# Gated mix of a long convolution and dilated local attention: x's first piece, the value weights and v loaded in other pieces, with a new written-out order

## The chip, the cores and the metric

The kernel runs on one core of a Trainium2 chip. A core has a matrix engine (TensorE, PE in the views; its weight loads are PEld), three engines for elementwise work (VectorE or DVE, ScalarE or ACT, GpSimd or POOL), a queue engine (SyncE or SP), and 16 DMA engines that move data between the chip's memory and the core's 128-partition buffer. Every engine works through its own instructions strictly in program order and waits on semaphores; a DMA is issued by SP, ACT or POOL and raises a semaphore when it has landed. The metric is device microseconds of one execution, as the median of several runs.

## What is computed

```python
x = A_q                                           # (1, 2048, 640), bf16
g = sigmoid((x * gate_w).sum(-1, keepdims=True))
# a: k is convolved with 4 taps, multiplied by v, and convolved over all 2048 positions
kv = sum_t(k shifted by t * shift_k[:, t]) * v
y  = irfft(rfft(kv, 4096) * rfft(ssm_k, 4096))[:2048] + kv * ssm_D
a  = A_q * y
# b: 32 heads of 20, each position sees itself and 7 earlier ones, every second position
q, k_, v_ = split(x @ wqkv)
b  = softmax(q . k_[pos - 2 * (0..7)] / sqrt(20)) . v_ @ wo
out = g * a + (1 - g) * b
```

## The kernel before, in words

**Attention.** x is loaded transposed (`load_x`, line 291) into `xT`, positions split by parity `par` into two halves of 1024, since the window has a dilation of 2. Each `load_x` is one transposing DMA of 512 rows, so x comes in four pieces x00, x01, x10, x11. `vproj` (line 437) multiplies pieces of 121 positions by the value weights `Wv`, once for the first 16 heads (columns 0 to 319 of `Wv`, hf 0) and once for the other 16 (hf 1). `qkproj` makes queries and keys, evicts them to `stg`, and `fragger` issues small DMAs from POOL (line 537, `qb<-stg`, `kb<-stg`, here called fragments) that put the heads where `score_gen` needs them. `score_gen` (scores, exp on ACT) and `pv_gen` (weighted values, normalised on DVE, lines 597 and 600) go through eight groups of four heads.

**Long convolution.** The channels lie on partitions in four quarters `q` of 32 partitions; partition 32q+p holds positions 64p to 64p+63 of the channels that start at CH[q] (CH = 0, 320, 160, 480). A quarter's 160 channels are two halves `c` of 80. k is loaded by eight DMAs into `kin`, v by eight DMAs into `vin[32q:32q+32, c]` (one for each q and c), the long filter by sixteen into `h_lin`. `conv` (line 410, its products on line 401 and its sums on line 408) is the 4-tap convolution on DVE, in place in `kin`. `conv_v` (line 426) then multiplies it by v in four DVE instructions, two for c = 0 and two for c = 1, on all 128 partitions: those of one c wait for all loads of that c. After that come two matmul stages for h and for kv (`transform`: `s1_unit`, line 621, and `s2_unit`, line 637), the product in the frequency domain (`products`), two inverse stages and the gating.

**Order.** All instructions are written out in an order made beforehand: `ORDER` is a string in which each letter lets one generator (a = `loads`, b = `fragger`, g = `conv_v`, v and w = `vproj` for the two halves of heads, and so on) emit its next request; `ENGINES` says which engine takes an eviction that ACT or DVE could take. The numbers in the requests (durations, landings, `plan.at`) are what the search for the order used; at run time they do nothing. An engine's queue follows the order even when a later instruction could already run.

**Pacing.** The loads of v and of the long filter are `paced` (line 286): POOL writes one element per partition of the destination first (line 288), and the DMA waits for that. So the place of that memset among POOL's fragments sets when SP may issue the load, and everything behind it on SP waits too. SP's order in `loads` (line 298) is x00, x01, W0 (query weights), x10, W1 (key weights), x11, eight k, eight v, sixteen h. The DMA of v on line 283 has this source, four times for each c:

```python
raw(v2, CH[q] + 80 * c, [[64 * D, 32], [D, 64], [1, 80]])      # [step, count], outermost first
```

The same helper builds the source of `g_nat` (line 466), the four small loads that spread the gate's row over partitions: `[[32 * pt, 2], [32, 16], [1, 32]]` for 32 destination partitions.

`heads` (line 357) emits what comes before the ordered part: two DMAs on ACT's queue for `Wv` (128-row blocks 0 to 2, then 3 and 4), `mm` (the mask rows), `ident` (for the transposes on line 755), the copies of the mask rows into key set 0 and query set 0 (`masks`, lines 354 and 355) on ACT, memsets on DVE, twelve warm-up matmuls, and small loads on POOL, `F` last among them.

Of the kernel before, what the change touches and what calls it, by code (L numbers as in the profile page):

```python
# [17 lines left out]
S = 2048  # L18
D = 640
# [7 lines left out]
BQ = 114  # L27
# [3 lines left out]
PRE = 7  # L31
X0 = 16
HS = 1024
HP = HS + 16
# [11 lines left out]
QC = 160  # L46
CR = 11
WARM = 12
CH = [0, 320, 160, 480]
# [61 lines left out]

STREAMS = "abcdefghijklmnopqrstuvwxyzABCDEFGHIJKLMNOPQRSTUVWXYZ"
ORDER = """
aaaaaaaaaaavwwwvvwvvvwwwvfaiviwvwviiiaweaiwvwvveeiibeiibwbwevveeivieeewwvvewbbbbbbbbbabwaeiiicecbibieecieccceacibcbcacbiebiacceccibbaidbcicc
bccbbbcabeediaieeiicbccbcbcciceicbbdccaabebcidccbbcaccdbeicccicdeieeabccccidbiacdcbceibcccecacieiciccbbbbbdbabbbacacaeccaaaadaicibabccbcacec
cddicicccecceeiiebieicbeacacecdcaceccibbdbddibiabeccciacjbjbccaggcbciabbcigacciccbcjccdicgcajjjaclcidbcihdccacbdccickialczzzccczacczckzzzccd
cczdzbbbbbbzbbbbbccbjazzczcccazbcacdbdcczzccczczkczzdccccczcjdczccczczkccaaazcazdaaacckcdkczcclzzczklzzzmzkzccdcAzccdzczAAAAAAAdAdnAAAzAzzAz
AAAAAABAppCpBBBABBABBBBBAABBCCBBBBkkkkkkkBkBBoABACAACCCCCAAAAAAAAAAACACACAoCCoCoCoooBoCopBooCoooCpCpCBpBBpCxBBpCCCxBxppCqCxBBxBBBqoBBqoCBBCo
xCBBBxxxxoCxxqqqqqxqkBCBCxxCxCqqCokxxxooooooooxxxoCCDykCCCCCqqqqqqqrqyqqrrrrDDrDDDDDDDyDDDDDyyDyDDyyyyyyyyyyyyyryyysDDEErEEEErrDEEEEEssErrEE
rrrrEsEEEEEskEsqqrrrtrttttttttttttttttttttttttttttttqqtstqttqqqqttqtstttttqqttuuuuuuuuuuuuuuuuuuuuuuuuuuuu  # L120
"""
ENGINES = """
DADADAADADDDADDAAAAADAAADAAAAAAADDAADADAAAADDDDDDDADADDDDADDDDDAADADADAADAADDAADADAADADADADADAADADADADADADADADADADAADAAADAADADADAAAAADAAADAA
AAAAAAAAAAAAAAADAAADAAADDDADDADADDAADAADASSSSSSSSSSSSSSSSSSSSSASSASAS
"""


# [50 lines left out]
def kernel(  # L178
# [14 lines left out]
    nc = tc.nc  # L193
# [6 lines left out]
    def raw(ap, off, dims):  # L200
        return bass.AP(tensor=ap.tensor, offset=ap.offset + off, ap=dims)
# [9 lines left out]
    plan = Plan(4)  # L211
# [48 lines left out]
    def ev(name):  # L260
        if name not in E:
            E[name] = Ev()
        return E[name]

    def mark(name, g):
        x = ev(name)
        x.t, x.eng = g.done.t, g.done.eng

    def at(name, t):
        ev(name).t = t  # L270
# [10 lines left out]
    def load(name, dst, src, us, deps=()):  # L281
        g = yield Req("S", 520.0, deps, move=us)
        nc.sync.dma_start(dst, src)
        mark(name, g)

    def paced(name, dst, src, us, deep=False):
        g = yield Req("G", 200.0)
        nc.gpsimd.memset(dst[:, 0, 0, 0:1] if deep else dst[:, 0, 0:1], 0.0)
        yield from load(name, dst, src, us, [g.done])

    def load_x(par, h, us):
        g = yield Req("S", 2700.0, move=us)
        nc.sync.dma_start_transpose(xT[:, :, X0 + HP * par + 512 * h:X0 + HP * par + 512 * h + 512],
                                    raw(x2, (1024 * h + par) * D, [[2 * D, 512], [1, D]]))
        mark(f"x{par}{h}", g)

    def loads():
        yield from load_x(0, 0, 5200.0)
        yield from load_x(0, 1, 4400.0)
        yield from load("W0", Wqk[:, :, 0, :], W3[:, :, 0, :], 2800.0)  # L300
        yield from load_x(1, 0, 2600.0)
        yield from load("W1", Wqk[:, :, 1, :], W3[:, :, 1, :], 3900.0)
        yield from load_x(1, 1, 3700.0)
        for c in (1, 0):
            for q in range(4):
                yield from load(f"k{q}{c}", kin[32 * q:32 * q + 32, 3 + 32 * c:35 + 32 * c, :],
                                raw(k2, 32 * c * D + CH[q], [[64 * D, 32], [D, 32], [1, QC]]), 2000.0)
        for c in range(2):
            for q in range(4):
                yield from paced(f"v{q}{c}", vin[32 * q:32 * q + 32, c], raw(v2, CH[q] + 80 * c, [[64 * D, 32], [D, 64], [1, 80]]), 2450.0)  # L310
        h_lin = p0.tile([128, 80, 2, 64], BF, name="h_lin", tag="HL")
        st["h_lin"] = h_lin
        for P in range(2):
            for q in range(4):
                for c in range(2):
                    yield from paced(f"h{P}{q}{c}", h_lin[32 * q:32 * q + 32, PL * P:PL * P + PL, c, :],
                                     raw(A_ssm_k, (CH[q] + 80 * c + PL * P) * S, [[64, 32], [S, PL], [1, 64]]), 1200.0)
# [37 lines left out]
        copier(qsets[e][:].rearrange("p (b k) -> p b k", k=BQ), mm[:, BK:BK + BQ].unsqueeze(1).to_broadcast([128, NB, BQ]))  # L355

    def heads():
        nc.scalar.dma_start(Wv[:, 0:3], W3[:, 0:3, 2, :])
        nc.scalar.dma_start(Wv[:, 3:5], W3[:, 3:5, 2, :])
        nc.scalar.dma_start(mm[:], ca["mm"].ap())  # L360
        nc.scalar.dma_start(ident[:], ca["ident"].ap())
        masks(nc.scalar.copy, 0)
        z = pab[:, 0].rearrange("p n c -> p (n c)")
        nc.vector.memset(z, 0.0)
        nc.vector.memset(ETall[:, :, :, 3 * BQ:], 1.0)
        nc.vector.memset(VW[:, :, :, DH], 1.0)
        for j in (0, NBP):
            nc.vector.memset(VW[0:PRE, j, :, DH], 0.0)
        wu = psp.tile([128, 2, 512], F32, name="wu", tag="ps0")
        for n in range(WARM):  # L370
            nc.tensor.matmul(wu[:, n % 2, :], lhsT=z[:, 0:128], rhs=z[:, 0:512], start=True, stop=True, skip_group_check=True)
        nc.gpsimd.memset(wgz[:], 0.0)
        nc.gpsimd.memset(xT[:, :, 0:X0], 0.0)
        for c in range(2):
            nc.gpsimd.memset(xT[:, :, X0 + HP * c + HS:X0 + HP * (c + 1)], 0.0)
        nc.gpsimd.dma_start(wgz[:, :, 0], gate_w.rearrange("(t p) -> p t", p=128))
        nc.gpsimd.memset(Dz[:], 0.0)
        for q in range(4):
            nc.gpsimd.dma_start(Dz[32 * q:32 * q + 1, :], raw(A_ssm_D, CH[q], [[0, 1], [1, 160]]))
        for q in range(4):  # L380
            nc.gpsimd.memset(kin[32 * q:32 * q + 1, 0:3, :], 0.0)
            nc.gpsimd.dma_start(wraw[32 * q:32 * q + 32].rearrange("p c j -> p (c j)"), raw(A_shift_k, 4 * CH[q], [[0, 32], [1, 4 * QC]]))
        masks(nc.gpsimd.tensor_copy, 1)
        for q in range(4):
            for a, b in ((1, 17), (17, 32)):
                nc.gpsimd.dma_start(kin[32 * q + a:32 * q + b, 0:3, :], raw(k2, (64 * a - 3) * D + CH[q], [[64 * D, b - a], [D, 3], [1, QC]]))
        nc.gpsimd.dma_start(F[:], cf["F"].ap())
        plan.at["A"] = 13500.0
        plan.at["G"] = 18500.0
        plan.at["P"] = 5500.0  # L390
        at("Wv0", 6500.0)

    def xdeps(par, i0, i1):
        return [ev(f"x{par}{h}") for h in range(2) if i0 < 512 * h + 512 and i1 > 512 * h]

    X4 = [f"x{par}{h}" for par in range(2) for h in range(2)]

    def taps(eng, n, m, ta, tb, dst):
        def tap(d, j):
# [24 lines left out]
    def conv_v():  # L424
        for c in range(2):
            for n in (0, 32):
                g = yield Req("D", 150.0 + 0.525 * 32 * 80, [ev("convD")] + [ev(f"v{q}{c}") for q in range(4)])
                nc.vector.tensor_tensor(vin[:, c, n:n + 32, :], kin[:, n + 3:n + 35, 80 * c:80 * c + 80], vin[:, c, n:n + 32, :], ALU.mult)
        mark("convV", g)

# [4 lines left out]
    def vproj(hf):  # L435
        for u in range(NBP):
            pieces = [divmod(2 * u + i, NBP) for i in range(2)]
            g = yield Req("P", 5 * 270.0, [d for par, j in pieces for d in xdeps(par, BQ * j - PRE, min(HS, BQ * j + BQ))] + [ev("Wv0")], take=1, mode="f", mm=10)
            ps = psum(g, "psv")
            for i, (par, j) in enumerate(pieces):  # L440
                s0 = X0 + HP * par + BQ * j - PRE
                for dt in range(NDT):
                    nc.tensor.matmul(ps[0:BK, i, 0:320], lhsT=xT[:, dt, s0:s0 + BK], rhs=Wv[:, dt, 320 * hf:320 * hf + 320],  # L443
                                     start=(dt == 0), stop=(dt == NDT - 1))
            r = yield Req("AD", n=640, deps=[g.done], give=g.banks)
            copy(r.eng, VW[0:BK, 2 * u:2 * u + 2, 16 * hf:16 * hf + 16, 0:DH], ps[0:BK, :, 0:320].rearrange("p a (h d) -> p a h d", d=DH))
            for i in range(2):
                mark(f"VW{2 * u + i}h{hf}", r)
        mark(f"vproj{hf}", g)

    def gate():
        g = yield Req("P", 1300.0, [ev(x) for x in X4], take=1, mode="g", mm=20)
        gps = psum(g, "gps", (128, 512))
        for dt in range(NDT):
            for c in range(4):
# [431 lines left out]
```

## Time and profile before

| what | us |
|---|---|
| median of 3 runs (236.31 to 237.9) | 236.75 |
| the profiled execution's own time | 235.22 |
| its span, first to last instruction | 233.1 |
| PE, DVE, ACT, POOL busy | 208.3, 184.5, 168.9, 58.7 |
| first `vproj` matmul | 10.68 |
| v's first and last load issued by SP | 47.2, 78.9 |
| first and last product of `conv_v` on DVE begin | 97.9, 103.7 |

All views are of one profiled execution; times in them count from the span's start. A busy share is over the span or a stretch. "Granted clock" (PEclk) is the share of TensorE's full clock that the chip allowed. In a line of the timeline the first number is the start, the second the time that the entries merged in it reach over.

### The profile page before, as it was taken

How to read it: one execution, taken by the hardware profiler on the slowest of the kernel's cores; microseconds unless marked ns; L12 is line 12 of the kernel's file. 1: busy time of each engine (PE TensorE's matmuls, PEld its weight loads, DVE VectorE, ACT ScalarE, POOL GpSimd, SP SyncE). 2: the span in 40 equal slices, each digit the busy share in tenths (PEclk: the TensorE clock that was granted, in tenths of full speed). 3: DMA queues.
4: the chain of work that ended last, by engine and by line, in shares of the span. 5: the costliest groups of instructions: out<-in, count | busy, mean ns of one | idle time of the engine just before them, and what ended most of it. 6: DMA issues, size and time to landing. Idle time of an engine off the chain costs nothing.

```text
span 233.1 us, 8740 instructions
## 1 busy us (share of the span) xinstructions
PE 208.3 (89%) x3802; PEld 168.2 (72%) x3802; DVE 184.5 (79%) x256; ACT 168.9 (72%) x216; POOL 58.7 (25%) x136
## 2 busy tenths in 40 slices
PE   6299999999899989999899998999999999997930
PEld 2189888866667656666667777888898999996920
DVE  4112269769999999997887779999999999598970
ACT  2432214459798989697999779998997979859950
POOL 8799030445733740742600000000000000000000
PEclk9769999999999999999855589999999999999995
DMA  7999999179699699978699550964767642294754
GB/s 190 221 269 294 167 165 158 36 160 166 115 142 171 128 148 144 145 111 190 119 177 195 172 183 18 211 146 88 172 141 164 158 107 40 56 236 84 184 128 95
DMA packets 74213, 34.91 MB, mean 150 GB/s; under 512 B 59876, under 2 KB 70768, under 8 KB 74176
## 3 DMA queue, kind: packets, MB, share of 16 engines
q1 hardware_dynamic: 69152, 27.50, 62.5%
q0 software_dynamic: 3792, 5.81, 11.9%
q10 hardware_dynamic: 1232, 1.06, 1.9%
q8 instruction: 29, 0.48, 0.9%
q14 instruction: 8, 0.07, 0.1%
HBM read 18.43 MB, written 2.62 MB: 90 GB/s over the span
## 4 chain that ended last, share of the span: by engine, by line
PE 49%; DVE 19%; DMA 10%; issue 9%; ACT 6%; POOL 3%; DVEq 0%; POOLq 0%; ACTq 0%
PE psv L443 10%; PE i L737 8%; PE op L775 7%; PE pj L492 7%; PE s L637 7%; DMA kb<-stg 6%; ACT ETall L567 4%; PE sc L560 4%; DVE Hs L207 4%; DMA wgz<-in_gate_w_dram 3%; DVE UC L207 3%; PE O L588 3%; DVE SX L835 3%; DVE SX L838 3%; PE tr L755 2%
## 5 line engine op out<-in xcount | busy, mean ns | idle before, releaser
L567 ACT ACTIVATE ETall<-sc 121x912 bf16<-121x912 f32 (+1 forms) x80 | 63.9, 863 | 9.2 <-PE sc L560 8.8
L492 PE MATMUL pj<-xT,Wqk 128*128 128x342 bf16 (+1 forms) x300 | 48.3, 310 | 2.6 <-ACT ETall L567 1.2
L492 PEld LDWEIGHTS <-Wqk 128*128 128x128 bf16 x300 | 28.4, 97 | 16.7 <-issue 2.2
L443 PE MATMUL psv<-KX,xT 128*121 128x320 bf16 x180 | 27.9, 318 | 4.2 <-POOL kb L353 4.2
L205 ACT CAST UC<-s 128x960 bf16<-128x960 f32 (+2 forms) x31 | 28.0, 982 | 3.7 <-PE s L637 2.2
L443 PEld LDWEIGHTS <-xT 128*121 128x121 bf16 x180 | 25.8, 144 | 6.0 <-POOL kb L353 4.7
L537 POOL DMA_DIRECT2D qb<-stg x36 | 18.0, 503 | 36.7 <-ACT stg L205 13.0
L401 DVE TENSOR_TENSOR KX<-KX 128x1760 bf16<-128x1760 bf16 (+1 forms) x24 | 24.6, 1044 | 0.5
L205 ACT CAST stg<-pj 128x726 bf16<-128x726 f32 (+1 forms) x17 | 12.8, 758 | 15.7 <-PE pj L492 12.7
L560 PE MATMUL sc<-qb,kb 31*128 31x114 bf16 x576 | 22.7, 229 | 1.6 <-DVE SX L207 0.5
L775 PE MATMUL op<-wo,oT 128*32 128x320 bf16 x640 | 23.9, 302 | 0.1
L637 PEld LDWEIGHTS <-SX 64*128 64x128 bf16 x512 | 20.9, 101 | 3.1 <-issue 2.3
L775 PEld LDWEIGHTS <-oT 128*32 128x32 bf16 x640 | 21.3, 140 | 1.3 <-issue 0.4
L537 POOL DMA_DIRECT2D kb<-stg x36 | 17.9, 502 | 17.0 <-issue 9.7
L560 PEld LDWEIGHTS <-kb 31*128 31x128 bf16 x576 | 13.8, 100 | 11.0 <-issue 9.2
L207 DVE CAST stg<-pj 128x684 bf16<-128x684 f32 (+1 forms) x13 | 11.5, 885 | 11.6 <-PE pj L492 9.2
L408 DVE TENSOR_TENSOR KX<-KX 128x1760 bf16<-128x1760 bf16 (+1 forms) x18 | 18.8, 1043 | 0.3
L207 DVE CAST SX<-s 128x1024 bf16<-128x1024 f32 (+1 forms) x13 | 15.2, 1191 | 3.7 <-PE s L637 2.9
L737 PE MATMUL i<-F,Hw 128*128 128x128 bf16 x160 | 18.0, 219 | 0.0
L737 PEld LDWEIGHTS <-Hw 128*128 128x128 bf16 x160 | 17.9, 113 | 0.0
L588 PEld LDWEIGHTS <-ETall 121*128 121x128 bf16 x576 | 16.2, 97 | 2.3 <-issue 1.0
L588 PE MATMUL O<-VW,ETall 121*128 121x21 bf16 x576 | 17.2, 174 | 0.5 <-DVE stg L207 0.4
(73 smaller groups left out, 339.3 us busy)
## 6 DMA issues: line engine op xcount, KB each, us to landing
KX<-in_A_k_dram SPq DMA_DIRECT2D x8, 320.0 KB
vin<-in_A_v_dram SPq DMA_DIRECT2D x8, 320.0 KB
h_lin<-in_A_ssm_k_dram SPq DMA_DIRECT2D x16, 160.0 KB
Hw<-SX SPq DMA_DIRECT2D x8, 320.0 KB
Hw<-Hs SPq DMA_DIRECT2D x8, 320.0 KB
SX<-in_A_q_dram SPq DMA_DIRECT2D x16, 160.0 KB
kb<-stg POOLq DMA_DIRECT2D x28, 85.1 KB, 3.9
qb<-stg POOLq DMA_DIRECT2D x28, 80.2 KB, 4.7
```

The costliest lines, as they stand in the source:

```text
L205: nc.scalar.copy(dst, src)
L207: nc.vector.tensor_copy(dst, src)
L401: eng.tensor_tensor(d, kin[:, n + 3 - j:n + 3 - j + m, :], w.to_broadcast([128, m, QC]), ALU.mult)
L443: nc.tensor.matmul(ps[0:BK, i, 0:320], lhsT=xT[:, dt, s0:s0 + BK], rhs=Wv[:, dt, 320 * hf:320 * hf + 320], start=(dt == 0), stop=(dt == ND ...
L492: nc.tensor.matmul(ps[:, i, 0:n], lhsT=Wqk[:, dt, w, 128 * ft:128 * ft + 128], rhs=xT[:, dt, s0:s0 + n], start=(dt == 0), stop=(dt == NDT ...
L537: nc.gpsimd.dma_start(dst[r0:r0 + rows, 0:wd], stg[fa - f0:fb - f0, 0:wd])
L560: nc.tensor.matmul(sc[:, hh, BQ * bb:BQ * bb + BQ], lhsT=kb[r:r + DH + NF, BK * b:BK * b + 128], rhs=qb[r:r + DH + NF, BQ * b:BQ * b + BQ] ...
L567: nc.scalar.activation(ETall[0:BK, e, :, 0:BQ * nb], sc[0:BK, :, 0:BQ * nb], ACT.Exp, scale=SCALE)
L588: nc.tensor.matmul(O[:, (b - b0) // 6, c0:c0 + 21], lhsT=ETall[0:BK, e, hh, BQ * bb:BQ * bb + 128], rhs=VW[0:BK, b, 4 * t + h4, :], start= ...
L637: nc.tensor.matmul(ps[:, c, 160 * jj:160 * jj + 160], lhsT=st["G"][rows, j0 + jj, rr, :], rhs=Am[rows, rr].rearrange("p o (q j) l -> p j ( ...
L737: nc.tensor.matmul(d, lhsT=st[(key, P)][:, c, o + il // 4, :, il % 4], rhs=M[:, k, :], start=(k == 0), stop=(k == 1), skip_group_check=True)
L775: nc.tensor.matmul(op[c:c + 32, tt, 0:320], lhsT=oT[:, ft, h, 32 * e:32 * e + 32, a], rhs=wo[:, ft, 320 * w:320 * w + 320], start=(ft == 0 ...
```

## The change

x00 becomes two transposing loads of 256 rows each (x00 and x01; the former x01 is now x02, the former x11 is x12). `Wv` is loaded by halves of heads, columns 0 to 319 first, and `vproj` waits only for its own half. The masks of set 0 are copied on DVE instead of ACT, behind DVE's memsets; `ident` is loaded from POOL's queue, after `F`, instead of ACT's. v comes in four transfers instead of eight, each for two quarters (64 partitions), and the source of each is written with the two quarters outermost. The planned durations, landings and `plan.at` are set anew, and `ORDER` and `ENGINES` come from a new search: 939 letters instead of 946, in `ENGINES` 114 A and 70 D instead of 110 and 74.

```diff
-    def load_x(par, h, us):
-        g = yield Req("S", 2700.0, move=us)
-        nc.sync.dma_start_transpose(xT[:, :, X0 + HP * par + 512 * h:X0 + HP * par + 512 * h + 512],
-                                    raw(x2, (1024 * h + par) * D, [[2 * D, 512], [1, D]]))
-        mark(f"x{par}{h}", g)
+    def load_x(name, par, t0, n, cost, us):
+        g = yield Req("S", cost, move=us)
+        nc.sync.dma_start_transpose(xT[:, :, X0 + HP * par + t0:X0 + HP * par + t0 + n], raw(x2, (2 * t0 + par) * D, [[2 * D, n], [1, D]]))
+        mark(name, g)
...
-        yield from load_x(0, 0, 5200.0)
-        yield from load_x(0, 1, 4400.0)
-        yield from load("W0", Wqk[:, :, 0, :], W3[:, :, 0, :], 2800.0)
...
+        yield from load_x("x00", 0, 0, 256, 2000.0, 2800.0)
+        yield from load_x("x01", 0, 256, 256, 2400.0, 3000.0)
+        yield from load_x("x02", 0, 512, 512, 4800.0, 4000.0)
+        yield from load("W0", Wqk[:, :, 0, :], W3[:, :, 0, :], 2400.0)
...
         for c in range(2):
-            for q in range(4):
-                yield from paced(f"v{q}{c}", vin[32 * q:32 * q + 32, c], raw(v2, CH[q] + 80 * c, [[64 * D, 32], [D, 64], [1, 80]]), 2450.0)
+            for q in (0, 2):
+                yield from paced(f"v{q}{c}", vin[32 * q:32 * q + 64, c], raw(v2, CH[q] + 80 * c, [[320, 2], [D, 2048], [1, 80]]), 3500.0)
...
     def heads():
-        nc.scalar.dma_start(Wv[:, 0:3], W3[:, 0:3, 2, :])
-        nc.scalar.dma_start(Wv[:, 3:5], W3[:, 3:5, 2, :])
+        for hf in range(2):
+            nc.scalar.dma_start(Wv[:, :, 320 * hf:320 * hf + 320], W3[:, :, 2, 320 * hf:320 * hf + 320])
         nc.scalar.dma_start(mm[:], ca["mm"].ap())
-        nc.scalar.dma_start(ident[:], ca["ident"].ap())
-        masks(nc.scalar.copy, 0)
...
+        masks(nc.vector.tensor_copy, 0)
...
         nc.gpsimd.dma_start(F[:], cf["F"].ap())
+        nc.gpsimd.dma_start(ident[:], ca["ident"].ap())
...
-                g = yield Req("D", 150.0 + 0.525 * 32 * 80, [ev("convD")] + [ev(f"v{q}{c}") for q in range(4)])
+                g = yield Req("D", 150.0 + 0.525 * 32 * 80, [ev("convD")] + [ev(f"v{q}{c}") for q in (0, 2)])
```

In the new order the four v loads are issued behind 13, 16, 32 and 37 requests of `fragger`; the eight of before behind 13, 17, 21, 27, 32, 37, 41 and 50. The four products of `conv_v` stand behind 80, 85, 87 and 93 requests of `score_gen`; before, behind 86, 86, 89 and 97.

More of the change, by code (lines that the diff above doesn't have):

```diff
@@ L113 @@
 ORDER = """
[L114 to L120, printed above, removed]
+aaaaavaaaaavvvawaawawvwvawvvwwviivvwiiwiiiiwiwwbeibeeeewwevewbvwibiwvvbbbebvbvvebeibwbabaiiiieicbbcaceecciecccbiifaiecbccbcbebiicccdccbcbbcb
+bibbecbbedbiibeideccciadeciccceicbeicacccicicccedccecebcdbbiibacbccabbadeccbbcccicdiccacbicbicccdccbbcicbceeeeedeicbabacdiecdcbbiccciaeeiaea
+becccaaabbeicaacbabaiccdccbaccajaicabebeeebjiibdgdciclabccadbbbiicbgccabaagbiccjjcjccliicgcaccjdhbickcccicdizaczcazbccdaccdczacaccbabzzbbbcb
+bcbbbbbzbczzzaacdcclzccccdzczcdcczckcdclckzzczczczzzccdccdczczzczkkczzkccczczcczzmzzzkczdccccdczzcAccAAAckdkcAccdczAAzAAzkzAdAdAAAAAAAnAAzBB
+AzBBBBoBAACBBkAABABAAAAAAApBABAAAACAABkCApBpCCCCCkCCCCCCCCCCCCBCBBBBABCooooACCCBBBBBoCBCpooooooBooxpBjBkBxjBBppxppppBkBBCooBBCxCqxkBxCxqqxoq
+CBqCBBqxoxxBxoxxxqxxxxoxxqqCCCCCCqxqqCCqCooqqoqCqqoqoooDokDDyyyDyDyDkyDkDrDyDyyDDyDyyDDDyyyyryDyyrrDyyyDDrErDErrErEsErEEtEEkssErEEErErrrsrEE
+rrrEEEsEqsEqttttttttttttttrtttttttqttqqttttuttttqttutuuuusqqsqqqtttqtttttqqttuuuuuuuuuuuuuuuuuuuuuu
 """
 ENGINES = """
-DADADAADADDDADDAAAAADAAADAAAAAAADDAADADAAAADDDDDDDADADDDDADDDDDAADADADAADAADDAADADAADADADADADAADADADADADADADADADADAADAAADAADADADAAAAADAAADAA
-AAAAAAAAAAAAAAADAAADAAADDDADDADADDAADAADASSSSSSSSSSSSSSSSSSSSSASSASAS
+AADDAAADDADAAADDAAAAAAAAADAADAAAADADAAAADAAAADDDDDDADDDDADADDDDADDADADADAADADADADADADADAADADADADADADADAADADADADADADAADAAADADADAAAADAAAAAAAAA
+AAAAAAAAAAAAAADAADAAADDADDAADDDADASASSSSSDAADDASSSSSSSSSSSSSSSSASSAAS
 """
@@ L289, in paced @@
         yield from load(name, dst, src, us, [g.done])
-    def load_x(par, h, us):
-        g = yield Req("S", 2700.0, move=us)
-        nc.sync.dma_start_transpose(xT[:, :, X0 + HP * par + 512 * h:X0 + HP * par + 512 * h + 512],
-                                    raw(x2, (1024 * h + par) * D, [[2 * D, 512], [1, D]]))
-        mark(f"x{par}{h}", g)
-    def loads():
-        yield from load_x(0, 0, 5200.0)
-        yield from load_x(0, 1, 4400.0)
-        yield from load("W0", Wqk[:, :, 0, :], W3[:, :, 0, :], 2800.0)
-        yield from load_x(1, 0, 2600.0)
-        yield from load("W1", Wqk[:, :, 1, :], W3[:, :, 1, :], 3900.0)
-        yield from load_x(1, 1, 3700.0)
+    def load_x(name, par, t0, n, cost, us):
+        g = yield Req("S", cost, move=us)
+        nc.sync.dma_start_transpose(xT[:, :, X0 + HP * par + t0:X0 + HP * par + t0 + n], raw(x2, (2 * t0 + par) * D, [[2 * D, n], [1, D]]))
+        mark(name, g)
+    def loads():
+        yield from load_x("x00", 0, 0, 256, 2000.0, 2800.0)
+        yield from load_x("x01", 0, 256, 256, 2400.0, 3000.0)
+        yield from load_x("x02", 0, 512, 512, 4800.0, 4000.0)
+        yield from load("W0", Wqk[:, :, 0, :], W3[:, :, 0, :], 2400.0)
+        yield from load_x("x10", 1, 0, 512, 4800.0, 2900.0)
+        yield from load("W1", Wqk[:, :, 1, :], W3[:, :, 1, :], 2600.0)
+        yield from load_x("x12", 1, 512, 512, 4800.0, 4400.0)
         for c in (1, 0):
@@ L306, in loads @@
                 yield from load(f"k{q}{c}", kin[32 * q:32 * q + 32, 3 + 32 * c:35 + 32 * c, :],
-                                raw(k2, 32 * c * D + CH[q], [[64 * D, 32], [D, 32], [1, QC]]), 2000.0)
+                                raw(k2, 32 * c * D + CH[q], [[64 * D, 32], [D, 32], [1, QC]]), 1950.0)
         for c in range(2):
-            for q in range(4):
-                yield from paced(f"v{q}{c}", vin[32 * q:32 * q + 32, c], raw(v2, CH[q] + 80 * c, [[64 * D, 32], [D, 64], [1, 80]]), 2450.0)
+            for q in (0, 2):
+                yield from paced(f"v{q}{c}", vin[32 * q:32 * q + 64, c], raw(v2, CH[q] + 80 * c, [[320, 2], [D, 2048], [1, 80]]), 3500.0)
         h_lin = p0.tile([128, 80, 2, 64], BF, name="h_lin", tag="HL")
@@ L387, in heads @@
         nc.gpsimd.dma_start(F[:], cf["F"].ap())
[L388 to L391, printed above, removed]
+        nc.gpsimd.dma_start(ident[:], ca["ident"].ap())
+        plan.at["A"] = 4500.0
+        plan.at["D"] = 10500.0
+        plan.at["G"] = 19000.0
+        plan.at["P"] = 6000.0
+        at("Wv0", 6000.0)
+        at("Wv1", 9800.0)
+    XP = {"x00": (0, 0, 256), "x01": (0, 256, 512), "x02": (0, 512, 1024), "x10": (1, 0, 512), "x12": (1, 512, 1024)}
     def xdeps(par, i0, i1):
-        return [ev(f"x{par}{h}") for h in range(2) if i0 < 512 * h + 512 and i1 > 512 * h]
-    X4 = [f"x{par}{h}" for par in range(2) for h in range(2)]
+        return [ev(x) for x, (p, a, b) in XP.items() if p == par and i0 < b and i1 > a]
     def taps(eng, n, m, ta, tb, dst):
@@ L437, in vproj @@
             pieces = [divmod(2 * u + i, NBP) for i in range(2)]
-            g = yield Req("P", 5 * 270.0, [d for par, j in pieces for d in xdeps(par, BQ * j - PRE, min(HS, BQ * j + BQ))] + [ev("Wv0")], take=1, mode="f", mm=10)
+            g = yield Req("P", 5 * 270.0, [d for par, j in pieces for d in xdeps(par, BQ * j - PRE, min(HS, BQ * j + BQ))] + [ev(f"Wv{hf}")], take=1, mode="f", mm=10)
             ps = psum(g, "psv")
@@ L451, in gate @@
     def gate():
-        g = yield Req("P", 1300.0, [ev(x) for x in X4], take=1, mode="g", mm=20)
+        g = yield Req("P", 1300.0, [ev(x) for x in XP], take=1, mode="g", mm=20)
         gps = psum(g, "gps", (128, 512))
```

## The prediction

> **What bounds the kernel now.** I read the page first (shares, slices), then the busy time by stretches, then the lines of the tiles that the change touches.
>
> ```profile
> PE 208.3 (89%) x3802; PEld 168.2 (72%) x3802; DVE 184.5 (79%) x256; ACT 168.9 (72%) x216; POOL 58.7 (25%) x136
> ...
> DVE  4112269769999999997887779999999999598970
> ...
> PEclk9769999999999999999855589999999999999995
> ```
>
> The reader is to see that PE is busy nearly throughout and that DVE is full from slice 7 to 18. The stretches say the same in us:
>
> ```profile
> 10.00:16.00 6.00, 5.32 (x21) 4.52 (x22) 0.00 (x0) 3.67 (x3) 5.96 (x8) 0.51 1.15 299
> 36.00:41.00 5.00, 5.00 (x38) 4.16 (x36) 4.86 (x5) 2.70 (x4) 0.00 (x0) 1.00 1.08 150
> 62.50:63.50 1.00, 1.00 (x21) 0.59 (x22) 1.00 (x2) 0.41 (x2) 1.00 (x3) 1.00 1.00 172
> 97.00:102.00 5.00, 4.86 (x78) 2.76 (x73) 5.00 (x6) 5.00 (x7) 0.49 (x2) 1.00 0.88 129
> ```
>
> Columns: stretch, length, busy time of PE, PEld, DVE, ACT, POOL, granted clock, DMA share, GB/s. At 97 to 102 us PE, ACT and DVE are all full: a wait in DVE's queue there has nothing to hide in. Two timelines (SP's, DVE's) and the tile views show what stands there:
>
> ```profile
> 10.68 13.62 PE L443 MATMUL psv<-KX,xT 128*121 128x320 bf16 x80 [4.19 <-POOL kb L353]
> ...
> 20.65 14.06 SPq L283 DMA_DIRECT2D KX<-in_A_k_dram  x8
> 47.22 32.22 SPq L283 DMA_DIRECT2D vin<-in_A_v_dram  x8
> 80.42 15.32 SPq L283 DMA_DIRECT2D h_lin<-in_A_ssm_k_dram  x8
> ...
> 97.88 2.89 DVE L428 TENSOR_TENSOR vin<-KX,vin 128x2560 bf16<-128x2560 bf16 x2
> ...
> 101.46 1.49 DVE L428 TENSOR_TENSOR vin<-KX,vin 128x2560 bf16<-128x2560 bf16 x1
> ```
>
> v is issued from 47.2 on; its landings in the trace's semaphore records end at 85.2. DVE's first product with v for c = 0 begins at 97.9, for c = 1 at 101.5: 13 to 16 us of slack, and SP's loads of the long filter stand behind v. How many DMA engines a load gets shows in its landings: each engine that carries a part raises the semaphore once.
>
> ```profile
> L466 SPq DMA_DIRECT2D g_nat<-KX x4: 501/546/680, 99.1 to 101.4; - x4
> ```
>
> These four loads have a source whose outermost count is 2 and 32 destination partitions. In the semaphore records each has three entries: one when SP finishes the issue and two landings (100.21, then 102.16 and 102.17 for the first). Loads with an outermost count of 32 or 128 on both sides have 16 landings. So g_nat's loads ran on two engines.
>
> **v in transfers of 64 partitions.** Removed: four SP issues (0.56 us and up) and four POOL memsets (0.09). Nothing waits for these, so nothing is gained. Moved: the last v issue comes before fragment request 38 instead of 51; v was not late, so this is worth nothing. Added: the new source counts [2, 2048, 80] against 64 partitions, outermost 2 as in g_nat's, where v's had 32 on both sides. By that row each transfer goes to two engines, the same two. The Trainium skill, "DMA: Bandwidth & Descriptors", section on why a DMA increments its semaphore by 16, states it as a rule: the engine count is the largest up to 16 that divides both sides' slowest counts, and on SP's queue the lowest-numbered engines are taken; here 2, and g_nat's two landings agree.
>
> The price. A v packet is 160 bytes; 16,384 of them in all, now 8,192 on each of two engines instead of 1,024 on each of 16. Pace of one engine, from the packet records: 14 ns median of one; 11.6 ns in the fastest half microsecond (63.0 to 63.5, where the stretch above gives 172 GB/s, or 14.9 ns over the whole of it); 18.2 ns as the mean of all 16,384, beside fragments. I take 14: 8,192 x 0.014 = 114.7 us; ends 95.0 and 149.1. The first packet came 1.7 us after the issue (48.94 after 47.22). Fragments share the engines: 758 packets of 4.1 to 4.4 KB between 46 and 92 us, 47 per engine, at 160 to 310 ns, are 7.6 to 14.7 us; I take 10. v's first issue stays behind the same 13 fragment requests: 47.2, less about 2 for the earlier start below, 45.
>
> So v lands at 45 + 1.7 + 114.7 + 10 = 171.4 us. DVE comes to the first c = 0 product at about 97 and waits to about 114 for the second transfer, and at the c = 1 product, due at 101.5, until 171.4. Behind it in DVE's queue are evictions of keys and queries and the normalisations of `pv_gen`; these hold PSUM and staging, so PE, then ACT and POOL, stop within some us. After that product 233.1 - 101.5 = 131.6 us remain.
>
> What is late next: the filter loads stand behind v on SP and in the two engines' queues. Eight of 160 KB are 80 packets of 128 bytes per engine, 13 ns each: 1 us a load, 8 to 9 us in all; h's first matmul came 8.4 us after the c = 1 product (109.9), and POOL's `Dz` addition (0.57) lies between: 2 us late (0 to 4). PE stands for tens of us; after its 4.2 us wait at the start the granted clock was 0.51 until 16 us, and 21 matmuls took 5.3 us where 38 take 5.0 at full clock: 2.5 us lost there, so I add 2 (0 to 2.5). The low clock at 112 to 137 may fall away after a long pause; PE was 4.4 to 5.0 busy of 5 there, but at less than twice the pace later: up to 8 us less, taken as 0 since no row shows it.
>
> **Start.** x00's packets: the 1,280th of 2,560 began at 5.95, the last at 7.98, and it landed at 10.59, after which PE began. A half piece would land at 7.3 to 8.6 (1.3 us as x01 lagged, or 2.6 as x00 did), so PE begins 2.0 to 3.3 earlier and may keep its clock (the 2.5 us above). Against it: one more transposing issue on SP, with no row of its own; at worst it delays all later loads by x00's lag, 2.6 us, and the taps of `conv` (34.9 us) wait for k behind it. DVE, full from 36 on, starts no earlier than k lands. Between +2.6 and -5.8; I take -2, and it is already in the 45 above.
>
> **Edits priced at nothing.** `Wv` by halves: its two loads landed at 4.48 and 6.58, before x00 in any case; if a packet of 640 bytes took the 55 ns of one of 1,280, the first half would land when both did, 6.6, and the second, read later, 2.2 us after. Masks on DVE: 2.01 and 1.90 leave ACT; DVE idles 9.3 us ahead of its first eviction at 16.18, and `mm` lands at 9.15. Without that cover an eviction waits up to 3.9 us, with PSUM's four buffers to carry it. `ident` on POOL: 0.57 us ahead of 3.9 us of masks, while POOL then idles 9.7 us; it is read at 144.7. The order and `ENGINES`: four evictions go from DVE to ACT (0.83 against 0.70 us each), under 1 us either way beside the 70 us wait.
>
> **Sum.** 171.4 + 131.6 + 2 + 2 = 307.0 us of span; the profiled execution's own time lies 2.1 over its span (235.22 against 233.1): 309. The median before is 1.5 over that execution; that is small beside the ends, and I leave it out.
>
> **Rivals.** A: v still spreads over 16 engines because the 64 partitions decide; then this ends on the other side. Place: v's landings; price: the start alone, 235.2 - 2 = 233, within 1% or a little better. It decides if each v load posts 16 landings. For it: v's own lines show no load of this form; against it: g_nat's 32 partitions did not decide. The Trainium skill's page named above, under its rules for kernel authors, advises one larger transfer over two on parts of the partitions, since these share the same 16 engines; by that rule too the merge would cost nothing, which is A's 233; no run here shows it yet.
> B: two engines, but a lone pair drains faster, since 14 others no longer compete. At 7 ns: 57.3 us, v at 114, 114 + 131.6 + 2 + 2.1 = 250. Against it: the fastest half microsecond is 11.6 ns, and filter packets of 128 bytes never went below 10.3. The wait vanishes only if v is in by 101.5, at 5.5 ns.
> C: two engines at the slow pace, 18.2 ns, and 14.7 us for fragments: 45 + 1.7 + 149.1 + 14.7 = 210.5, + 131.6 + 4 + 2.1 = 348. It is the upper end of the forecast, not a case of its own.
>
> **Numbers.** Two engines at 11.6 to 18.2 ns: 0.84, 309 us the likeliest. Low end: v at 45 + 1.7 + 95 + 7.6 = 149.3, + 131.6 + 2.1 = 283, less the 8 of the low clock = 275, and 274 is given; high end 348. That range holds some 0.95 of the case, 0.8 of all. A: 0.11, of which 0.05 faster by over 1% (about what a measurement of this kernel tells from no change) and 0.06 within 1%. B: 0.05, slower. Faster 0.05, same 0.06, slower 0.89.
>
> **What would show it.** Right: two landings per v load; SP issues of v that last tens of us; a wait of DVE on `conv_v` (line 428) for the DMA of v of 60 us or more, all engines idle in one block between about 100 and 170 us with the DMA share near 2/16; PE beginning at 7.5 to 9. Wrong: 16 landings per v load, or v landed by 100 us.

## The result and the profile after

The changed kernel takes 314.19 us (median of four runs, 310.96 to 321.76) where the kernel before takes 236.53: a ratio of 1.317, 95% interval 1.305 to 1.329. The ratio is taken from the two shorter of these runs (310.96 and 312.38 us), since the two others lie more than 1.5% above the shortest. The profiled execution took 312.38 us with a span of 310.6. The forecast was 309 (274 to 348), slower.

Busy shares and slices on the page of the changed kernel:

```profile
PE 216.1 (70%) x3802; PEld 171.0 (55%) x3802; DVE 185.3 (60%) x254; ACT 168.7 (54%) x219; POOL 60.7 (20%) x133
...
DVE  4303789949889004000003507877999989986991
...
PEclk9999999969989776655555555557999999999997
DMA  8999954414333311111117999560088968518373
```

DVE did the same work as before (185.3 us against 184.5) in a span 77 us longer. Counted from 0, its slices 13 to 20, about 101 to 163 us, are empty but for one, and from slice 14 on the DMA share there is 1 tenth: something moves, on few engines. The busy time by stretches of the changed kernel (stretch, length, PE, PEld, DVE, ACT, POOL, granted clock, DMA share, GB/s):

```profile
106.00:116.00 10.00, 3.19 (x26) 1.63 (x25) 0.17 (x1) 3.73 (x5) 0.00 (x0) 0.67 0.16 28
...
146.00:156.00 10.00, 0.00 (x0) 0.00 (x0) 0.00 (x0) 0.00 (x0) 0.00 (x0) 0.50 0.18 25
...
176.00:186.00 10.00, 2.15 (x52) 1.60 (x49) 0.96 (x2) 2.68 (x3) 6.44 (x16) 0.50 1.08 144
186.00:196.00 10.00, 8.13 (x178) 6.35 (x179) 8.20 (x10) 7.58 (x10) 1.38 (x4) 0.50 0.93 159
196.00:206.00 10.00, 9.67 (x185) 7.12 (x188) 7.63 (x10) 8.31 (x11) 0.57 (x1) 0.50 0.47 153
```

At 146 to 156 no engine does anything, and 25 GB/s arrive at a DMA share of 0.18: two engines of sixteen would be 0.125, but packets in flight overlap (from 115.7 us on a packet's record lasted 17.9 ns on average, and each engine began one every 12.7), and 2/16 x 17.9/12.7 is 0.18. Before, with v under way at 62.5 to 63.5 us, it was 172 GB/s at a share of 1.00. What everyone waits for stands in the view of `vin` and in SP's and DVE's timelines of the changed kernel:

```profile
L283 SPq DMA_DIRECT2D vin<-in_A_v_dram x4: 723/29391/36842, 42.9 to 114.0; - x4
L430 DVE TENSOR_TENSOR vin<-KX,vin x4: 1478/1486/1493, 115.8 to 170.2; 128x2560 bf16<-128x2560 bf16 x4
...
  DMA vin<-in_A_v_dram: 62.5, 2
```

```profile
42.88 97.36 SPq L283 DMA_DIRECT2D vin<-in_A_v_dram  x4
140.33 37.22 SPq L283 DMA_DIRECT2D h_lin<-in_A_ssm_k_dram  x11
177.65 1.86 SPq L468 DMA_DIRECT2D g_nat<-KX  x3
```

```profile
115.83 1.49 DVE L430 TENSOR_TENSOR vin<-KX,vin 128x2560 bf16<-128x2560 bf16 x1 [14.18 <-DMA vin<-in_A_v_dram]
...
167.95 1.49 DVE L430 TENSOR_TENSOR vin<-KX,vin 128x2560 bf16<-128x2560 bf16 x1 [48.33 <-DMA vin<-in_A_v_dram]
...
185.61 1.23 DVE L207 CAST SX<-s 128x1024 bf16<-128x1024 f32 x1 [9.04 <-DMA g_nat<-KX]
```

DVE waits 14.2 us for the c = 0 transfers and 48.3 for c = 1. The semaphore records hold, for each v load, one entry of SP and two landings (the first: 43.98, then 81.19 and 85.63); before it was sixteen. SP itself is held: the second, third and fourth issue of v last 37, 33 and 26 us where an issue of v lasted 0.6 to 2.1, and the first filter load behind them 25.6 us, so the filter loads and the gate's row behind it are late too, which is the 9.0 us on the last line.

### The profile page after: what moved, and what is told of

Same layout as the page of the kernel before. It is cut to its first block, busy times and chain, and to the rows that moved or that the text cites. A ratio compares the mean times of both kernels' runs of the same rounds, so it can differ in the third digit from the quotient of the medians.

```text
span 310.6 us, 8726 instructions
## 1 busy us (share of the span) xinstructions
PE 216.1 (70%) x3802; PEld 171.0 (55%) x3802; DVE 185.3 (60%) x254; ACT 168.7 (54%) x219; POOL 60.7 (20%) x133
## 4 chain that ended last, share of the span: by engine, by line
PE 37%; SPq 23%; DMA 14%; DVE 9%; issue 8%; ACT 5%; POOL 2%; POOLq 0%; DVEq 0%; ACTq 0%
SPq L283 22%; PE psv L445 8%; PE pj L494 7%; PE s L639 5%; PE i L739 5%; PE op L777 4%; DMA qb<-stg 4%; PE sc L562 4%; DMA xT<-in_A_q_dram 3%; DVE Hs L207 2%; ACT ETall L569 2%; DVE UC L207 2%; PE O L590 2%; PE s L623 2%; DMA g_nat<-KX 2%
## 5 line engine op out<-in xcount | busy, mean ns | idle before, releaser
L494 PE MATMUL pj<-xT,Wqk 128*128 128x342 bf16 (+1 forms) x300 | 55.6, 342 | 11.4 <-DVE oS L602 9.1
L590 PE MATMUL O<-VW,ETall 121*128 121x21 bf16 x576 | 17.5, 176 | 46.7 <-DVE stg L207 46.2
L494 PEld LDWEIGHTS <-Wqk 128*128 128x128 bf16 x300 | 30.7, 105 | 30.1 <-issue 12.1
L430 DVE TENSOR_TENSOR vin<-KX,vin 128x2560 bf16<-128x2560 bf16 x4 | 5.9, 1486 | 62.5 <-DMA vin<-in_A_v_dram 62.5
L205 ACT CAST UC<-s 128x960 bf16<-128x960 f32 (+2 forms) x33 | 30.0, 981 | 2.3 <-PE s L639 1.8
L205 ACT CAST stg<-pj 128x684 bf16<-128x684 f32 (+1 forms) x19 | 14.0, 746 | 29.1 <-PE pj L494 16.3
L207 DVE CAST SX<-s 128x1024 bf16<-128x1024 f32 (+2 forms) x17 | 19.8, 1168 | 12.9 <-DMA g_nat<-KX 9.0
L445 PE MATMUL psv<-KX,xT 128*121 128x320 bf16 x180 | 25.5, 299 | 2.1 <-DMA xT<-in_A_q_dram 1.3
L445 PEld LDWEIGHTS <-xT 128*121 128x121 bf16 x180 | 24.0, 134 | 3.7 <-DMA xT<-in_A_q_dram 1.6
L539 POOL DMA_DIRECT2D kb<-stg x36 | 18.0, 504 | 12.7 <-ACT stg L205 7.9
L205 ACT CAST VW<-psv 121x640 bf16<-121x640 f32 x14 | 9.4, 697 | 18.3 <-PE psv L445 18.1
L207 DVE CAST stg<-pj 128x726 bf16<-128x726 f32 (+1 forms) x11 | 9.9, 899 | 15.8 <-PE pj L494 14.2
```

The lines of the kernel that those rows point to most:

```text
L205: nc.scalar.copy(dst, src)
L207: nc.vector.tensor_copy(dst, src)
L494: nc.tensor.matmul(ps[:, i, 0:n], lhsT=Wqk[:, dt, w, 128 * ft:128 * ft + 128], rhs=xT[:, dt, s0:s0 + n], start=(dt == 0), stop=(dt == NDT ...
L539: nc.gpsimd.dma_start(dst[r0:r0 + rows, 0:wd], stg[fa - f0:fb - f0, 0:wd])
L590: nc.tensor.matmul(O[:, (b - b0) // 6, c0:c0 + 21], lhsT=ETall[0:BK, e, hh, BQ * bb:BQ * bb + 128], rhs=VW[0:BK, b, 4 * t + h4, :], start= ...
```

## The experiments

Theory E: a load runs on as many DMA engines as both sides' outermost counts allow, here two; v, waited for by DVE, is the whole loss. Rival O: the new order and the landings it was planned for cost the time. Rival M: the merging does, 640 KB under one wait. The ratios below are against the kernel before, run beside each on the same chip.

**e1_v32.** The changed kernel with each merged load cut back into two:

```diff
-raw(v2, CH[q] + 80 * c, [[320, 2], [D, 2048], [1, 80]])        # into 64 partitions
+for r in (q, q + 1): raw(v2, CH[r] + 80 * c, [[64 * D, 32], [D, 64], [1, 80]])   # into 32 each
```

> The changed kernel with its new order, but each v transfer of 64 partitions issued as two of 32 whose source has 32 outermost, at the same place. Theory E (a load runs on as many engines as divide both sides' outermost counts, so v ran on two): v lands by about 80 us, no wait of DVE for v, 230 to 236 us. Rival O (the new order and the planned landings cost the time, v's form does not): stays at 305 to 315. Rival M (it is the merging, 640 KB on 64 partitions under one wait): 230 to 236 too.

Measured: 238.52 us, 1.011 (1.005 to 1.018); v landed by 78 us, sixteen landings a load, no wait for v. Everything else of the change was in it, so O is refuted as the cause of the 77 us. The time is above the 230 to 236 expected: a remainder of 1% above before stays, and e8 and e11 look for it.

**e2_outer2, e3_outer4, e4_outer8.** The kernel before with only the way its v sources are written changed, for the same bytes:

```diff
-raw(v2, CH[q] + 80 * c, [[64 * D, 32], [D, 64], [1, 80]])
+raw(v2, CH[q] + 80 * c, [[16 * 64 * D, 2], [D, 1024], [1, 80]])     # e3: 4 and 512, e4: 8 and 256
```

> The kernel before, order and eight transfers untouched; only the source of each v load is written with outermost count 2 (two times 1,024 rows) for the same bytes and partitions. Theory E: 8,192 packets of v on each of two engines, at 17.6 ns beside fragments and 12.7 ns alone (as the changed kernel's records show), land near 165 us; 305 to 318 us. Rivals O and M: nothing that they name is changed, 235 to 238.

> The kernel before with outermost count 4 in v's source (four times 512 rows). Theory E: 4,096 packets on each of four engines at 17.6 ns, 72 us, land near 121 us (115 if the pace recovers while DVE waits), 14 to 20 us after DVE's product at 101.5; with what is late behind it 250 to 265 us. Rivals O and M: 235 to 238.

> The kernel before with outermost count 8 in v's source (eight times 256 rows). Theory E: 2,048 packets on each of eight engines, 36 us at 17.6 ns, about what the pacing already spreads them over; v lands by 90 us, before DVE asks at 97.9: 235 to 238 us, the same. Rivals O and M: 235 to 238 as well; this run only tells whether E's slack of some 13 us is right.

Measured: 237.25, 236.47 and 236.63 us; 1.004 (0.999 to 1.009), 1.002 (0.996 to 1.007), 1.000 (0.994 to 1.006). Two expectations of E missed, and the records say why: every v load still has sixteen landings. The step between the two outer counts is exactly the inner count times its step (16 x 64 x D = 1,024 x D), so they are one run of rows, and I take it that they were issued as such. (That the source's counts do not matter at all is no way out: `g_nat`'s loads and the merged v loads have 32 and 64 partitions, and two landings.) So the edit did not change how many engines ran and tells E and its rivals nothing apart; e4's time, inside its range, says nothing either. What the three do show: a written count of 2, 4 or 8 was harmless where its step joins the next. In the changed kernel it can't join: its step is 320 elements, half a row.

**e5_four_rows and e10_many_loads.** A count that can't be joined, without merging anything. Both are the kernel before with each v load issued as eight loads of 40 KB; e5 by partitions, e10 by positions:

```diff
+for r in range(0, 32, 4):                                                  # e5: four partitions a load
+    nc.sync.dma_start(vin[32 * q + r:32 * q + r + 4, c], raw(v2, 64 * r * D + CH[q] + 80 * c, [[64 * D, 4], [D, 64], [1, 80]]))
...
+for r in range(0, 64, 8):                                                  # e10: 32 partitions, eight positions
+    nc.sync.dma_start(vin[32 * q:32 * q + 32, c, r:r + 8], raw(v2, r * D + CH[q] + 80 * c, [[64 * D, 32], [D, 8], [1, 80]]))
```

> The kernel before, order untouched; each v load of 32 partitions issued as eight loads of 4 partitions at the same place (outermost count 4 on both sides, which cannot be merged away). Theory E: each of these runs on four engines, the lowest, so 4,096 packets of v on each; from 48.9 us at 17.6 ns beside fragments, then 12.7 ns while DVE waits: landed near 116 us, DVE waits some 14 us for c = 1, with the filter and the gate's row late behind it 250 to 265 us. Rival M (the merging to 640 KB under one wait): smaller loads, so no harm beyond 56 more issues of 0.56 us on SP, which the pacing hides: 236 to 242.

> The kernel before with as many v loads as the run with loads of 4 partitions, 64, and the same bytes in each, but each of 32 partitions and 8 positions, so 16 engines. Theory E (engines, not the number of issues, made that run 40 us slower): 236 to 242 us, v in by 95 us. Rival: 64 issues on SP cost it, then 260 to 278 here too.

Measured: e5 276.64 us, 1.164 (1.155 to 1.174); e10 240.57, 1.011 (1.004 to 1.018). The same 64 issues of the same 40 KB differ by 36 us (on two chips, each beside the kernel before). In e5 each load has four landings, v is in at 132 us instead of the expected 116, and DVE waits for it (first the waits of e5, then, from the view of `vin`, the issues of e5 and of e10):

```profile
DVE vin L433 <- DMA vin<-in_A_v_dram: 25.0, 1, 25.0
```

```profile
L314 SPq DMA_DIRECT2D vin<-in_A_v_dram x64: 614/962/3367, 46.5 to 128.4; - x64
```

```profile
L314 SPq DMA_DIRECT2D vin<-in_A_v_dram x64: 311/449/1932, 47.5 to 86.1; - x64
```

So few engines cost the time in transfers a sixteenth the size of the merged ones, and M is refuted as the only cause. A merged load that runs on sixteen engines was not built, so merging's own share, if it has one, is not measured. The size of e5 was above E's 250 to 265; its SP issues last twice as long as e10's and follow one another to the end, which the expectation had not counted.

**e6_wide_c1.** A dose: the kernel before with only c = 1 in the merged, two-engine form.

```diff
+if c == 0: the load of before
+elif q % 2: nc.sync.dma_start(vin[32 * q - 32:32 * q + 32, c], raw(v2, CH[q - 1] + 80 * c, [[320, 2], [D, 2048], [1, 80]]))
```

> The kernel before, order untouched; v for c = 0 as before, for c = 1 in two transfers of 64 partitions with outermost 2, at the places of the second and the fourth load. Theory E: two landings per wide transfer; 4,096 packets on each of two engines from about 70 us, 17.6 ns until DVE asks at 101.5, then 12.7 ns: landed near 132 us, a wait of some 30 us, 266 to 280 us, less than half of what four wide transfers cost. Rival O (the order): 235 to 238.

Measured: 272.63 us, 1.148 (1.139 to 1.158), inside E's range; the last v packets began at 129.4 (132 expected). DVE's wait was 21.5 us instead of 30, and the rest of the loss came behind it: the c = 1 product was 28.4 us later than before, and from it to the end took 6.7 us longer. On the old order, half of v in this form costs 36 us. The view of `vin` of e6:

```profile
L316 SPq DMA_DIRECT2D vin<-in_A_v_dram x2: 658/12285/23912, 68.9 to 78.7; - x2
...
  DMA vin<-in_A_v_dram: 21.5, 1
```

**e7_gate_row and e9_gate_act.** The 9.0 us wait behind v. A first eviction into SX overwrites the place that the gate's row is spread from, so it waits for the `g_nat` loads. Both are the changed kernel; e7 splits each of these four loads into two of 16 partitions, so that each runs on sixteen engines, e9 leaves them and issues them from ACT's queue:

```diff
-nc.sync.dma_start(g_nat[32 * gg:32 * gg + 32, :], raw(src, 64 * (gg // 2) * pt, [[32 * pt, 2], [32, 16], [1, 32]]))
+nc.scalar.dma_start(g_nat[32 * gg:32 * gg + 32, :], raw(src, 64 * (gg // 2) * pt, [[32 * pt, 2], [32, 16], [1, 32]]))   # e9
```

> The changed kernel, with the gate's row spread by eight loads of 16 partitions (outermost 16 on both sides) instead of four of 32 with outermost 2. My theory for what the prediction missed behind v: the 9.0 us that DVE waits before its first eviction into SX are the gate's row crawling through the two engines behind filter packets and fragments; with 16 engines the wait shrinks to under 3 us and the run takes 303 to 308 us. Rival: the wait is SP's order (the gate's row is issued behind eleven filter loads), then it stays near 9 us and 311 to 315.

> The changed kernel, with the four loads of the gate's row issued from ACT's queue instead of SP's, in the same two-engine form. The run with eight 16-engine loads ruled out the crawl through two engines (the wait of DVE before its first eviction into SX grew to 12.6 us). Theory now: the wait is SP's order, the gate's row is issued only when v and eleven filter loads are through; from ACT's queue it is done long before, the wait falls under 1 us, the stretch from the first c = 1 product to the end shrinks from 142.7 to some 135 us, and the run is 5 to 9 us shorter than the changed kernel (303 to 309 beside 311 to 315). Rival: the filter itself is late, then the wait moves to POOL's addition on the filter and nothing is gained.

Measured: e7 322.75 us, 1.350 (1.337 to 1.364); e9 314.08, 1.318 (1.308 to 1.328). Neither came to the 303 to 308 us or 303 to 309 us expected. The wait grew in e7 and shrank in e9 (DVE's timeline of each; in e7 the view names a filter load, but the row's last load landed at 198.13, just ahead):

```profile
198.40 1.23 DVE L207 CAST SX<-s 128x1024 bf16<-128x1024 f32 x1 [12.62 <-DMA h_lin<-in_A_ssm_k_dram]
```

```profile
186.00 1.23 DVE L207 CAST SX<-s 128x1024 bf16<-128x1024 f32 x1 [2.07 <-PE s L623]
```

My first theory, two engines for the gate's row, falls: from issue to landing the row's last load took 4.9 us on sixteen engines in e7 and 5.5 on two in the changed kernel, and e7's four added issues put it later, 21.0 us after the first c = 1 product instead of 17.5. What counted was the row's place on SP, behind the filter: in e9, away from there, its last load landed after 9.3 us. But e9's edit did not free the row from v, as its expectation had it. ACT came to the row's first load at 112.6 us and issued it only at 174.43, when v had landed; the records show that this load posts on the semaphore of v's last load and waits for it. ACT works in order, so four `exp` pieces stood behind it that the changed kernel had done by 125.6 us (ACT's waits in e9):

```profile
ACT ETall L569 <- DMA g_nat<-KX: 63.6, 1, 63.6
```

And the rest of DVE's wait went to h's first matmul, which waits for POOL's addition on the filter, as the rival had it. From the first c = 1 product to the end e9 takes 139.65 us (314.1 - 174.45) where the changed kernel takes 142.65, 3.0 less instead of 5 to 9, and the ratio to before is the same: v was in at 167.8 us in the changed kernel's profile, at 174.3 in e9's and 177.0 in e7's, and that spread between executions is as large as what was looked for (the profiled ones of e7 and e9, at 324.52 and 316.21 us, lie above their medians).

**e8_start and e11_all_but_v_order.** What the rest is worth: the kernel before, with its own order and v loads, and first x00 in two loads and `Wv` by halves (e8), then the masks on DVE and `ident` on POOL's queue as well (e11).

> The kernel before, order untouched; x00 in two loads of 256 rows, and the value weights by halves of heads (the first product still waits for both halves). If the start's gain reaches the end: PE begins at 7.5 to 8 instead of 10.7 and 233 to 234.5 us. If it is lost because DVE's taps are bound by k's landing: PE begins as early, 235.5 to 237. If the added transposing issue delays k: 237 to 239.

> The kernel before, its order and its v loads, with everything else of the change: x00 in two loads, value weights by halves of heads, masks of set 0 on DVE, ident from POOL's queue. If the new order is what costs the 1.1% that remained with v in 16-engine loads: 233 to 236 us, 0.985 to 0.995 of before. If one of these edits costs it: 238 to 240.

Measured: e8 234.92 us, 0.988 (0.980 to 0.997); e11 232.95, 0.981 (0.976 to 0.986). Both lie just outside what was expected, e8 above 234.5 and e11 below 233. e11 is faster than both kernels, 1.9% below before. The same edits under the new order, e1, were 1.1% above it: the new order costs some 3%, by one run each on two chips. In the profiles the cost lies ahead of v's product: the first c = 1 product begins at 103.84 us in e1 and 98.93 in e11, and from there to the end they take 132.68 and 132.43. Between 50 and 100 us PE's work differs most at 60 to 65 (e1, then e11):

```profile
60.00:65.00 5.00, 2.01 (x44) 1.48 (x43) 4.90 (x8) 1.74 (x3) 1.14 (x4) 1.00 0.98 155
```

```profile
60.00:65.00 5.00, 4.74 (x89) 3.23 (x87) 4.97 (x6) 4.48 (x6) 1.44 (x5) 1.00 1.12 184
```

PE has 2.01 us of work there against 4.74. In e1 the chain of waits between 57.1 and 63.2 us is a fragment (`qb<-stg`) under way. Whether a better order for these edits exists was not tried.

## Why the prediction was right, step by step

**Two engines for v: right.** Shown by the two landings, by the DMA share of 0.18, and by e1, e5, e6 and e10. The Trainium skill, "DMA: Bandwidth & Descriptors", section on why a DMA increments its semaphore by 16, says that the engine count divides both sides' slowest counts; two landings with an outermost 2, four with 4 and sixteen with 32 agree with it.

**When v is in: right, by luck in part, since two errors cancel.** Forecast 171.4, measured 167.8. The pace alone, taken as 14 ns, was 12.7: 14 was the median record of one packet, which it is here too, but the records overlap. The last 4,096 packets of each engine came in from 115.7 to 167.8 us, while no fragment ran. Beside fragments, the first 4,096 took from 44.5 to 115.7, 17.4 ns each; at 12.7 that leaves 19 us beyond v's own, where 10 were taken for the fragments. The fragments' own records in that stretch come to 14.8 us an engine, the upper bound given (14.7); what the other 4 us are is open. The sum was 124.7 against 123.3 measured. The rest of the 3.6 us is the earlier first issue, 42.9 instead of 45.

**DVE's waits: right.** c = 0 to about 114 (measured 115.8), 60 us or more in all (62.5). One reading was off, without effect on the sum: the slack of 13 us is counted from c = 1's last landing to the first product of c = 0, whose own loads had landed by 67.3 us, 31 us ahead of it.

**What remains after the product: 7 us too short.** Forecast 131.6 + 2 + 2, measured 142.65. The filter's 2 us late was right: h's first matmul began 10.7 us after the product (178.64), against 8.4 before. The step that was mis-sized is "what is late next": the gate's row, which stands behind the filter on SP, was not in it. e1 has the same order without the wait for v, so beside it the trace shows where the time goes (us after the first c = 1 product):

| | e1 | changed kernel |
|---|---|---|
| h's first matmul | 6.9 | 10.7 |
| first eviction into SX, behind the gate's row | 7.6 | 17.7 |
| kv's first matmul | 43.5 | 54.7 |
| end | 132.7 | 142.7 |

The changed kernel is 10.1 us behind at the eviction, 11.2 at kv's first matmul and 10.0 at the end: nearly all of it is lost before the eviction. The clock, priced at 2 us, stayed low far longer than the start had suggested (5 or 6 us): the trace's clock records have 0.50 from 126.0 to 211.4 us, which is until 41 us after PE had work again, and ten `pj` matmuls at 172.5 took 3.08 us instead of 1.65. But from the eviction to kv's first matmul, where the changed kernel was at half clock for 29 us and e1 for 20, the two differ by 1.1 us only. So the long low clock cost little behind the eviction; what it cost ahead of it, where DVE waits for the row, no run separates.

**The start: right in its place.** PE began at 7.74 us (2.0 to 3.3 earlier than 10.68 was forecast), and its clock was 1.00 to 16 us where it had been 0.51.

```profile
7.74 1.54 PE L445 MATMUL psv<-KX,xT 128*121 128x320 bf16 x10 [0.81 <-PE wu L370]
```

Its price of -2 us fits e8 (0.988, or 2.8 us). e11, at 0.981, holds the masks and `ident` as well; the two intervals overlap, so what these add is not shown. What the forecast missed lies in "the order, under 1 us either way": by e1 against e11 that is some 3%, 5 us in the profiles and 7 by the ratios, hidden here under the wait for v.

**The rivals.** A (sixteen engines) did not happen; e1, which makes it happen, took 238.52, not 233, for the order's sake. The advice of the Trainium skill ("DMA: Bandwidth & Descriptors", rules for kernel authors) of one larger transfer over two on parts of the partitions, which stood beside A, did not hold here: the larger one cost 32%, the two smaller kept v off the path (e1). Its premise, that both forms use the same 16 engines, was not met by the larger one, with its two landings. B (7 ns a packet) and C (18.2 throughout) are both out: alone it was 12.7, and 17.4 with the fragments already in it.

## What to carry to other kernels

When a DMA is merged or rewritten, look at the outermost count on both sides that is left after neighbouring counts have joined: in these runs it set how many DMA engines carried the load, and a merge that left a 2 there turned a load that was hidden into the wait that ends last. The landings per load show it in one look. The load that drained slowly held its issuing queue too, so name everything behind it there, down to the small transfers whose buffers others wait to overwrite. To price what is late behind a wait, compare with a run that has the same order and no wait, as e1 is here.

## What the runs showed that I had not expected

- The loads on two engines held SP's queue: the first issue of v lasted 0.72 us, the other three 26 to 37, and each ended at about the time when the load ahead of it had landed (the second at 81.3 us, the first load's landings at 81.2 and 85.6).
- Fragments from POOL's queue landed later in the changed kernel, though they move no more bytes: a median of 6.4 us for the 85 KB key fragments, against 3.9 before and 4.4 in e1. But e11, with v on sixteen engines, has 5.4, so it is not shown that v's form does it.
- The granted clock stayed at 0.50 until 211.4 us, though PE was busy 8.1 and 9.7 of 10 us from 186 on, and all of 206 to 211.
- The gate's row, put on ACT's queue in e9, held ACT from 112.6 to 174.4 us.
- A source written with an outermost 2 whose steps join with the next count ran on sixteen engines (e2), the same count with a step of half a row on two.
